# adaLN block with hedgehog attention and a gMLP: `c` moved to another DMA queue, the scale and shift columns reordered, the last output tile split by columns

## The chip, the cores and the metric

The kernel runs on one core of one Trainium2 chip. Its time is device microseconds, the median of the runs shown. The engines are named as in the profile: PE (TensorE matmuls) with PEld (its weight loads), DVE (VectorE), ACT (ScalarE), POOL (GpSimd) and SP (SyncE, which here only issues DMAs). A name with a q behind it (SPq, ACTq) is the engine's sequencer, which issues DMAs. In the lists of DMA packets q1 is the queue of DMAs issued by SP, and q10 that of DMAs issued by ACT.

## The reference

S = 2048 rows, D = 448, 16 heads of 28, FH = 896, all in bf16. Cut to what matters:

```
mod = silu(c) @ w_mod                       # c has 448 numbers; six vectors sa, ca, ga, sb, cb, gb
h   = layernorm(x) * (1 + ca) + sa
q, k, v = h @ wqkv ;  pq, pk = q @ w_phi, k @ w_phi        # per head
phi = [softmax(p), softmax(-p)]
o   = (phi_q @ (phi_k^T v)) / (phi_q . sum(phi_k))
x   = x + ga * (o @ wo)
h   = layernorm(x) * (1 + cb) + sb
z   = gelu(h @ w_in) ; z1, z2 = halves, z2 = layernorm(z2)
x   = x + gb * ((z1 * (w_sp @ z2 + b_sp)) @ w_out)
```

## The kernel before

x is cut into 16 tiles of 128 rows. The program is a list of small steps in the string `ORDER`: each word is one step, optionally with a PSUM slot behind `@` (A0 to A2, B0, B1) and an engine behind `/` (V is DVE, S is ACT, G is POOL, Y is SP). The steps are emitted in exactly that order, so each engine's own order of instructions is the order of the words that it takes part in, and an engine waits only where its next instruction needs something. `consts()` (memsets and the identity) is emitted ahead of the list.

The steps that the change and the prediction touch:

- `ld:c`, `ld:wk`, `ld:x1`, `ld:x0`, `ld:phi`, `ld:wsa`, `ld:wca`, `ld:wq`, `ld:wv`, `ld:x3`: DMA loads, of `c` (one row of 448), the raw key weights, the tiles 1 and 0 of x, w_phi, the columns of w_mod for sa and for ca, the raw query and value weights, the tiles 4 to 7.
- `du:n@slot`: n dummy matmuls of 256 columns on the tile `zero` (line 729). They compute nothing that is used.
- `ct`: turns the row `c` into four columns (four matmuls with one column, line 740). `ce:1` to `ce:4`: silu of it, an exponential on ACT (line 747), then three small operations on DVE (lines 749, 751, 753), which give `scol`.
- `FTk:1`, `FTk:0`: transposes of the key weights on PE (line 822), 8 each; `ETk:1`, `ETk:0`: the copies out of PSUM (826 on ACT, 828 on DVE); `bd`: block-diagonal w_phi on DVE (756); `PFk:m`: key weights times w_phi (849); `EPk:m`: their scaled copies (796, 800).
- `csA`: 16 matmuls of one column that give the shift columns sa from `scol` (764); `esA` copies them (771). `ccA` and `ecA` do the same for ca (764, 768). `FSk`: 16 matmuls of one column with the shift (839).
- `l1s:i`: layer-norm statistics of tile i on DVE (856, 857); `l1e`, `l1r` on POOL (860, 861, 864: epsilon, negated mean, power); `l1a:i`: the normalised tile in `xpad` (867); `X:i`: its four transposes on PE (880); `XE:i`: the copy to `hT`.
- At the end, `oM:t,0,7`: seven matmuls of 448 columns for output tile t (1159), alternately in B0 and B1; `oE:t`: the sum with x on DVE (1162); `oD:t`: the DMA to the output (1165), all on SP.

Behind the list stands a branch on a flag, which skips a general version of the kernel; it is not taken in these runs.

Of the kernel before, what the change touches and what calls it, by code (L numbers as in the profile page):

```python
# [481 lines left out]
ORDER = """tbl du:8@B1 m2b/V ld:wk/Y du:3@A2 m2a/V du:11@A1 ld:c/Y ct@B0 ld:x1/S l1s:1 ld:x0/S l1s:0 m1/G ld:phi/Y ce:1 m3 FTk:1@B1 ce:2 l1e:1,2/G ld:wsa/Y du:2@A0  # L482
l1e:0,1/G FTk:0@A0 ld:wca/Y ce:3 ce:4 bd/V ld:x2/Y ld:wq/Y l1r:0,1 l1a:0/V du:6@A2 X:0@B0 ETk:0/S csA@A2 ETk:1/V PFk:2@B1 l1r:1,2 esA l1a:1/G X:1@A0 XE:0/V
m4 du:2@A2 FSk@B0 ccA@A1 FCk/S PFk:0@B0 ecA XE:1/S EPk:0/V EPk:2/S l1s:3 du:1@A2 PFk:1@A1 EPk:1/S ld:wv/Y l1s:2 PFk:3@A0 l1e:2,4/V EPk:3/S du:2@B0 kM:1@B1
FTq:1@A2 ETq:1/V ld:x3/Y FTq:0@B0 ETq:0/V kM:0@A0 kF:1 FSq@A2 FCq/V kE:1 kS:1 PFq:1@B0 scb kF:0 kE:0 l1r:2,4 l1a:2/G l1a:3/G l1s:4 X:2@B1 SHv@A1 PFq:2@A2
SCv:1/G EPq:1/S XE:2/S l1s:6 PFq:0@B0 SCv:2/G X:3@A0 l1s:5 kM:2@B1 SCv:0/S XE:3/S l1s:7 ld:x4/Y l1s:9 EPq:0/S SCv:3/G l1e:4,8/G l1s:11 kS:0 vM:2@A1 vM:3@B0
EPq:2/S vC:2 ld:wmgb/Y kE:2 PFq:3@A0 EPq:3/S ld:wmga/Y l1s:8 kM:3@A2 kF:2 qM:1@A1 kR:1 ld:x5/S l1r:4,8 vM:0@B1 kR:0 kS:2 kE:3 kF:3 vM:1@A2 l1s:10 qE:1
l1a:4/G gr:1@A0 vC:0 l1s:13 l1a:5/G vC:1 ge:1 gr:0@B1 l1a:7/G kS:3 l1a:6/G vC:3 T1:4,6 kP:0/G T1:6,8 qF:1 kR:2 ge:0 qM:0@A2 qE:0 kP:1/G l1s:12 kM:5@B0
kM:4@B1 kF:4 kP:2/V vM:5@A1 kA:0@A0 kE:4 l1e:8,12/G l1r:8,12 kA:1@A0 kA:2@A0 ld:wo/Y vM:6@B1 l1a:8/G kF:5 kE:5 kR:3 kP:3/V l1s:14 l1s:15 kM:7@B0 l1a:9/G
qF:0 kS:5 vC:6 kM:6@A2 l1a:10/G kS:4 vC:5 l1a:11/G qM:2@A1 kF:6 kR:5 kF:7 kR:4 kE:6 kP:5/V ld:wcb/Y qF:2 T1:8,10 kP:4/V kS:6 kR:6 vM:7@B1 kE:7 T1:10,12  # L490
kA:3@A0 wos:0/G l1e:12,16/G vM:4@A2 l1r:12,16 vC:7 qE:2 l1a:15/G kM:9@B0 kF:9 l1a:12/V l1a:14/G kM:8@B1 l1a:13/V vM:9@A1 kE:9 kS:7 kR:7 kF:8 vC:4 kS:9
kE:8 kS:8 T1:12,14 kM:10@B0 kP:6/G kE:10 kP:7/G kR:8 kF:10 kA:4@A0 kA:5@A0 kM:11@B1 kE:11 T1:14,16 kS:10 vM:10@B0 kF:11 kS:11 kA:6@A0 vC:9 kA:7@A0 kM:12@B1
kP:8/G kR:10 kE:12 kR:9 kP:9/V kR:11 vC:10 kP:10/V kF:12 kS:12 kM:13@A1 kR:12 vM:8@A2 kM:15@B0 vC:8 kF:13 kP:11/G kM:14@B1 ld:wsb/Y kE:13 kS:13 kR:13 kE:14
W:0,6 kF:14 kE:15 kA:8@A0 kA:9@A0 kP:12/V kS:14 vM:11@A1 kF:15 kS:15 kA:10@A0 vM:14@B1 kR:14 vC:11 vM:15@B0 vC:14 vM:12@A2 vM:13@B1 vC:12 kA:11@A0 vC:13
kP:13/G kA:12@A0 kR:15 kP:14/V kP:15/V wos:2/V kA:13@A0 kA:14@A0 vC:15 kA:15@A0 KV:0/V KV:1/V KZ:0 ld:win0/S qM:3@A2 KZ:1 nM:0@A1 qE:3 ld:wout/S nM:1@A0
nX:0 nX:1 qF:3 nC:0 csB@B0 W:0,1 ld:win1/Y nC:1 nS:0 ccB@B1 nT:0 qM:4@A2 qE:4 nA:0/V nT:1 ecB nA:1/V wos:3/V qM:5@A1 nM:2@A0 qF:4 esB nX:2 nM:3@A2 nX:3
FB@B1 wos:1/V nC:2 qE:5 T2:0,1 nC:3 nS:1 FBc/S qF:5 nT:2 nA:2/G wM:0/S@B0 nT:3 SHw:3@B1 wR:0/S SCw:0,3/S T2:1,2 nM:5@A1 nX:5 nM:4@A0 nC:5 nX:4 nC:4 nA:3/V
wQ:0/S wM:1/S@B0 wR:1/S SHw:2@B1 SCw:2,1/S qM:6@A2 SCw:0,0/S SCw:3,1/G nS:2 nT:5 nT:4 T2:2,4 nM:6@A1 wQ:1/V qE:6 nX:6 nM:7@A0 nA:5/G nA:4/V nX:7 SCw:0,2/S
qF:6 nC:6 nC:7 nS:3 nT:7 wM:2/S@B0 wR:2/S wM:3/S@B1 wR:3/S qM:7@A2 wQ:2/S nT:6 wQ:3/S nA:6/V SCw:1,1/V SCw:1,0/V nM:9@A0 T2:4,6 qE:7 nM:8@A1 wM:5/S@B1
nX:8 nX:9 wM:4/V@B0 l2R:0,2/G l2r:0,2 l2a:0/G T3:0,1 l2a:1/V qF:7 nC:8 wR:5/S zM:0@A2 gt nA:7/G l2R:2,4/G nC:9 nS:4 nT:9 nT:8 zG:0 l2r:2,4 l2a:3/G T2:6,8  # L500
wR:4/V l2a:2/G nM:10@A0 T3:1,2 T3:2,4 wQ:5/S nX:10 nA:8/V SCw:3,0/G wM:6/V@B1 wR:6/V nM:11@A1 wQ:4/S nX:11 nA:9/V SCw:2,0/V l2R:4,6/G zM:1@A2 nC:11 nC:10
zG:1 l2r:4,6 nS:5 l2a:5/V wQ:6/S wM:7/V@B1 l2a:4/G yM:0,0@B0 zM:2@A2 yG:0,0 T2:8,10 nT:10 wR:7/V zQ:1/V T3:4,6 W:1,3 zM:3@A0 zG:2 wM:8/V@A2 wQ:7/S l2R:6,8/G
W:0,5 wM:9/V@B1 nT:11 nA:11/V nA:10/V zG:3 wR:8/V zQ:0/S nM:12@A0 nM:13@A2 l2r:6,8 l2a:6/G zM:4@A1 wR:9/V nX:13 nX:12 T2:10,12 zR:0,2/G zQ:3/S wQ:8/S W:1,7
yM:0,4@B0 zG:4 yM:0,1@B1 zQ:4/S nC:13 nM:15@A1 nC:12 zW:0,2 nX:15 yG:0,1 nS:6 nT:13 wQ:9/S nM:14@A2 nX:14 l2a:7/G nT:12 zN:0/V zM:5@A0 yG:0,4 T3:6,8 l2R:8,10/G
l2r:8,10 nA:12/V l2a:9/G nA:13/V nC:15 wM:11/V@B1 zG:5 nC:14 nS:7 l2a:8/G nT:14 zQ:5/S wR:11/V yM:0,5@B0 nT:15 yM:1,3@A0 T2:12,14 yM:1,0@A2 nA:14/G zQ:2/V
nA:15/V yG:0,5 zR:4,6/G zN:1/G wM:10/V@B0 zW:4,6 wM:13/V@A1 wM:12/V@B1 wR:13/V W:2,0 W:0,2 zN:5/G yG:1,0 yG:1,3 yM:1,4@A0 wR:12/V zR:2,4/V zW:2,4 zN:3/G
zN:2/V zM:6@A2 wQ:12/S yM:1,5@B1 wQ:13/S wR:10/V wQ:10/V zG:6 zM:7@A1 T2:14,16 W:2,6 wQ:11/S l2R:10,12/G l2R:12,14/V l2r:10,12 wM:15/V@B0 yG:1,5 zN:4/V
l2a:11/V yM:0,2@A2 wR:15/V zQ:6/S T3:8,10 yM:0,3@B1 W:1,4 W:0,0 zG:7 l2r:12,14 yM:1,1@A1 l2a:13/G yG:1,4 W:0,4 l2a:10/V T3:10,12 yG:1,1 yM:1,2@A0 l2a:12/V
wM:14/V@B0 yG:1,2 zQ:7/V zM:8@A1 yG:0,2 T3:12,14 wR:14/V wQ:14/V yG:0,3 zG:8 wQ:15/V l2R:14,16/V zQ:8/S zR:6,8/G zW:6,8 zN:7/G zM:9@A2 zG:9 zN:6/V l2r:14,16
W:1,1 yM:1,6@B1 yM:0,6@A1 yG:0,6 yG:1,6 zQ:9/V l2a:15/V zM:11@A0 yM:2,5@B0 zM:10@A1 l2a:14/V zG:11 guard@B1 zQ:11/V zG:10 zQ:10/S zM:12@A0 yM:2,4@B1 W:1,5  # L510
zR:8,10/G W:1,0 zG:12 zM:13@A2 zW:8,10 T3:14,16 zR:10,12/G zW:10,12 yG:2,5 yM:3,6@A0 zN:8/V yG:2,4 zN:9/V zG:13 yM:2,2@B1 yG:2,2 yG:3,6 zM:15@A1 yM:3,4@A2
W:1,2 W:2,2 zN:10/V zG:15 zQ:15/S zM:14@A0 zQ:13/V yG:3,4 zN:11/G zG:14 zQ:12/V zR:12,14/V yM:2,6@B0 yM:3,0@A2 yM:3,1@B1 W:1,6 yG:2,6 zQ:14/S tT:1,2/G
yG:3,0 yM:3,2@A0 yM:2,0@A1 zW:12,14 sS:0,1,0,8/V yM:2,1@B0 yM:2,3@A2 yG:3,2 yM:3,5@A0 tT:1,0/V yG:2,0 yG:3,1 zR:14,16/G zW:14,16 zN:14/V zN:15/V yM:3,3@A1
yG:3,5 zN:13/G tT:1,1/V yG:3,3 zN:12/V tT:3,0/V W:0,3 sS:0,2,0,8/V yG:2,3 W:0,7 tT:2,2/V tT:2,1/V ld:bsp/Y gM:1@B1 gG:1 gal P:0,0,1 d:0,0,2 P:0,1,1 tT:2,0/V
d:0,1,1 tT:4,0/V P:0,1,6 d:0,1,3 gM:0@B1 sS:0,3,0,8/V P:0,0,6 P:0,1,5 sS:0,4,0,8/V gG:0 P:0,0,7 d:0,0,1 d:0,0,3 P:0,0,2 d:0,0,4 x:0,0,4/G W:3,4 P:0,0,5
d:0,0,5 W:3,5 W:2,1 P:0,2,1 W:3,1 d:0,0,7 P:0,0,3 P:0,0,4 tT:3,2/V d:0,0,6 d:0,1,2 wts:0/V x:0,0,6/V d:0,0,8 W:2,4 d:0,1,5 wts:1/V x:0,0,8/V tT:3,1/V P:0,1,2
W:3,0 d:0,1,4 W:3,2 wts:2/V tT:4,2/G P:0,2,6 P:0,1,3 x:0,0,7/V wts:3/V d:0,2,1 d:0,2,3 W:2,3 W:2,7 d:0,2,2 x:0,1,4/G P:0,2,7 d:0,1,6 wts:4/V x:0,1,6/V
P:1,0,1 d:1,0,2 P:0,2,2 tT:4,1/V read P:0,2,5 W:3,6 W:2,5 W:3,7 P:0,1,7 d:0,2,4 wts:5/V W:3,3 P:1,1,1 d:0,2,5 wts:6/V P:0,2,3 x:0,2,4/G d:0,2,7 sS:1,1,0,8/V
yG:2,1 sS:1,2,0,8/V d:0,2,6 gM:3@B0 d:0,1,7 gG:3 P:0,1,4 P:0,2,4 x:0,2,7/V x:0,1,7/G d:0,1,8 x:0,2,6/V oM:0,0,7@B0 x:0,1,8/G oE:0 oD:0/Y oM:1,0,7@B1 d:1,1,1
P:1,0,6 d:1,0,1 oE:1 d:1,0,3 d:1,1,2 oM:3,0,7@B0 P:1,0,5 P:1,1,6 oE:3 sS:1,3,0,8/G P:1,0,7 oD:1/Y d:0,2,8 d:1,0,5 d:1,0,7 gM:2@B1 gG:2 P:1,0,2 P:1,1,2  # L520
oM:2,0,7@B1 P:1,0,4 x:1,0,7/V x:0,2,8/G d:1,0,4 P:1,2,1 x:1,0,4/G oM:5,0,7@B0 d:1,1,3 sS:1,4,0,8/V P:1,1,5 d:1,1,5 oE:5 oD:5/Y P:1,1,7 oE:2 d:1,0,8 P:1,0,3
oM:4,0,7@B0 d:1,1,7 d:1,0,6 x:1,0,6/G oD:2/Y d:1,2,1 P:1,2,6 oD:3/Y d:1,2,2 P:1,2,2 oM:6,0,7@B1 P:1,2,7 x:1,0,8/V d:1,2,3 oE:6 P:1,1,3 d:1,1,6 P:1,2,5
oE:4 oD:4/Y oD:6/Y x:1,1,7/G P:1,1,4 x:1,1,6/G oM:7,0,7@B0 d:1,1,4 x:1,1,4/G d:1,2,4 x:1,2,4/G hint d:1,2,5 P:1,2,3 d:1,2,7 d:1,2,6 oE:7 x:1,2,6/G P:1,2,4
d:1,2,8,256,512 oD:7/Y oM:9,0,7@B0 oE:9 oD:9/Y d:1,2,8,0,256 oM:8,0,7@B1 oE:8 x:1,2,7/G oD:8/Y oM:10,0,7@B0 d:1,1,8 oE:10 x:1,1,8/G oD:10/Y oM:11,0,7@B1
oE:11 oD:11/Y x:1,2,8,0,256/G oM:12,0,7@B0 oE:12 oD:12/Y oM:13,0,7@B1 oE:13 oD:13/Y x:1,2,8,256,512/G oM:14,0,7@B0 oM:15,0,7@B1 oE:14 oD:14/Y oE:15 oD:15/Y
# [741 lines left out]
```

## Time and profile before

| | |
|---|---|
| median of 3 runs | 250.34 us (249.0, 250.34, 250.72) |
| the profiled execution | 249.4 us, of which the span is 247.6 us |
| PE busy | 240.5 us, 97% of the span |
| DVE, POOL, ACT busy | 182.5, 116.3, 104.8 us |
| DMA | 25.22 MB, 102 GB/s on the mean |

The span runs from the first instruction to the last event on the core; the execution's own time is 1.8 us longer. PE is busy nearly throughout, so what delays or advances PE at the start moves what stands behind it, and what stands behind PE's last matmul (from 243.2 us on) is a tail in which PE has nothing to do.

### The profile page before, as it was taken

The page shows a single profiled execution, that of the slowest core. Times are in us where ns is not written, and L with a number is a line of the kernel's source. Part 1 is how long each engine was busy: PE and PEld are TensorE (multiplying, and loading weights), DVE is VectorE, ACT ScalarE, POOL GpSimd, SP SyncE. Part 2 cuts the span into 40 slices and gives each one's busy share as a digit, 9 for nine tenths or more (in the row PEclk, how much of TensorE's full clock was granted, in tenths as well). Part 3 has the DMA queues.
Part 4 walks back from the last instruction along what each step waited for, and adds up shares of the span by engine and source line. Part 5 has one row for each costly group of instructions (what it writes and reads, how often), then busy time and mean ns, then how long its engine had stood idle before and what let it go on. Part 6 is the DMA issues. An engine that isn't in the chain of part 4 may idle for free.

```text
span 247.6 us, 4188 instructions
## 1 busy us (share of the span) xinstructions
PE 240.5 (97%) x1533; PEld 126.8 (51%) x1533; DVE 182.5 (74%) x369; ACT 104.8 (42%) x217; POOL 116.3 (47%) x175
## 2 busy tenths in 40 slices
...
GB/s 178 293 217 102 193 86 177 194 113 178 51 72 110 127 162 136 163 158 176 179 177 0 162 181 173 0 1 0 3 0 37 0 0 3 56 0 37 21 95 65
DMA packets 68207, 25.22 MB, mean 102 GB/s; under 512 B 58129, under 2 KB 67602, under 8 KB 68178
## 3 DMA queue, kind: packets, MB, share of 16 engines
...
q8 instruction: 14, 0.23, 0.4%
...
## 4 chain that ended last, share of the span: by engine, by line
PE 85%; POOL 6%; ACT 3%; DVE 2%; DMA 1%; issue 1%; POOLq 0%
PE g_ps L1124 29%; PE o_ps L1159 9%; PE z_ps L1049 7%; PE q_ps L945 6%; PE k_ps L890 5%; PE v_ps L898 5%; PE g_ps L1145 5%; PE z_ps L1078 4%; PE x_ps L1005 4%; PE kvacc L921 3%; PE warm_ps L729 3%; PE num L973 2%; POOL f_zv L1035 1%; DMA f_hT<-f_xpad 1%; DVE f_z2n L1072 1%
## 5 line engine op out<-in xcount | busy, mean ns | idle before, releaser
L1133 DVE TENSOR_TENSOR f_zb<-g_ps,f_zb 128x512 f32<-128x512 f32 (+1 forms) x31 | 20.5, 670 | 17.1 <-PE g_ps L1124 16.7
L1124 PEld LDWEIGHTS <-f_z2n 128*128 128x128 bf16 x192 | 18.8, 98 | 22.7 <-issue 0.3
L1140 POOL TENSOR_TENSOR f_z1T<-f_zb,f_z1T 128x512 bf16<-128x512 f32 (+1 forms) x11 | 12.0, 1102 | 33.6 <-DVE f_zb L1133 33.6
L1049 PE MATMUL z_ps<-f_ar,f_hT 112*128 112x448 bf16 (+1 forms) x128 | 26.6, 352 | 0.0
L1140 POOL TENSOR_TENSOR f_z1T<-f_Sx,f_z1T 128x512 bf16<-128x512 f32 x6 | 8.0, 1332 | 39.3 <-DVE f_Sx L1133 39.3
L1078 PE MATMUL z_ps<-f_hT,f_ar 112*128 112x512 bf16 x112 | 26.1, 379 | 0.0
L1159 PE MATMUL o_ps<-f_wout,f_z1T 128*128 128x448 bf16 x112 | 22.5, 352 | 0.0
L1124 PE MATMUL g_ps<-f_ar 128*128 128x512 bf16 x96 | 22.4, 379 | 0.0
L1081 ACT ACTIVATE f_z1T<-z_ps,f_zb 128x512 bf16<-128x512 f32 x28 | 18.2, 684 | 5.2 <-PE z_ps L1078 5.1
L950 ACT ACTIVATE f_Eq<-q_ps 112x1024 bf16<-112x1024 f32 x16 | 16.3, 1032 | 5.8 <-PE q_ps L945 5.8
L1049 PEld LDWEIGHTS <-f_hT 112*128 112x128 bf16 (+1 forms) x128 | 12.2, 97 | 11.6
L1078 PEld LDWEIGHTS <-f_ar 112*128 112x128 bf16 x112 | 11.0, 98 | 12.6
L893 ACT ACTIVATE f_E<-k_ps 128x448 bf16<-128x448 f32 x32 | 15.8, 555 | 3.8 <-PE k_ps L890 3.7
L989 DVE TENSOR_TENSOR f_ar<-num,f_w 128x896 bf16<-128x896 f32 x16 | 17.0, 1087 | 0.4
L904 DVE TENSOR_REDUCE f_ksum<-f_E 128x32 f32<-128x896 bf16 x16 | 16.9, 1064 | 0.5 <-ACT f_E L893 0.4
L1124 PE MATMUL g_ps<-f_Eq,f_z2n 128*128 128x512 bf16 x72 | 16.5, 379 | 0.0
L1159 PEld LDWEIGHTS <-f_z1T 128*128 128x128 bf16 x112 | 11.0, 98 | 10.7
L1053 ACT ACTIVATE f_zb<-z_ps 128x896 bf16<-128x896 f32 x16 | 14.6, 913 | 4.1 <-PE z_ps L1049 3.8
L1162 DVE TENSOR_TENSOR f_xpad<-o_ps,f_x 128x448 bf16<-128x448 f32 x16 | 9.9, 622 | 8.0 <-PE o_ps L1159 7.9
L945 PE MATMUL q_ps<-f_hT,f_Wq 113*128 113x512 bf16 (+1 forms) x64 | 15.0, 379 | 0.6 <-ACT f_Eq L950 0.6
L1124 PEld LDWEIGHTS <-f_ar 128*128 128x128 bf16 x96 | 9.4, 98 | 11.1 <-DVE f_ar L1102 0.2
L1005 PE MATMUL x_ps<-f_ar 112*128 112x448 bf16 x64 | 14.1, 352 | 0.3 <-DVE f_x L1012 0.3
...
## 6 DMA issues: line engine op xcount, KB each, us to landing
out_dram<-f_xpad SPq DMA_DIRECT2D x16, 112.0 KB, 1.7
f_wm<-in_w_mod_dram SPq DMA_DIRECT2D x4, 406.0 KB, 5.1
f_x<-in_A_x_dram SPq DMA_DIRECT2D x2, 448.0 KB, 7.8
f_wmg<-in_w_mod_dram SPq DMA_DIRECT2D x2, 392.0 KB, 9.9
...
```

What stands on the lines that cost most here:

```text
L904: nc.vector.tensor_reduce(out=ksum[:, i], in_=Er[i % NR][:].rearrange("p s (c f h) -> p (s c) h f", c=4, h=HP), axis=AX.X, op=ALU.add)
L945: nc.tensor.matmul(t[:, u, :], lhsT=Wq[0:KR[m], m, cc * CB:cc * CB + P], rhs=hT[0:KR[m], 4 * st:4 * st + 4, m, :], start=(m == 0), stop=(m ...
L950: nc.scalar.activation(out=Eq[st // 2][0:CB, 2 * c2:2 * c2 + 2, s, (st % 2) * 512:(st % 2 + 1) * 512], in_=ps["q" + str(n)][0:CB, :, :], f ...
L989: nc.vector.tensor_tensor(out=tr[i % 2][:], in0=numv(i)[:, :, :, 0:DH], in1=wr[i // 2 % 2][:, i % 2].unsqueeze(3).to_broadcast([P, 2, H, D ...
L1005: nc.tensor.matmul(t[:, 0, 0:D], lhsT=oT[0:CB, i % 4, cc, :], rhs=wo_s[0:CB, cc, :], start=(cc == 0 and not with_x), stop=(cc == KC - 1))
L1049: nc.tensor.matmul(t[:, hf, 0:D], lhsT=hT[0:KR[m], i, m, :], rhs=win_s[0:KR[m], m, FH + hf * D:FH + (hf + 1) * D], start=(m == 0), stop=(m ...
L1078: nc.tensor.matmul(t[:, 0, :], lhsT=win_s[0:CB, m, fc * P:(fc + 1) * P], rhs=hT[0:CB, 4 * st:4 * st + 4, m, :], start=(m == 0), stop=(m == ...
L1081: nc.scalar.activation(out=stage_b()["z1T"][:, fc, st * 512:(st + 1) * 512], in_=ps["y%d_%d" % (st, fc)][:, 0, :], func=ACT.Gelu_apprx_tan ...
L1124: nc.tensor.matmul(g, lhsT=sta[:, m, :], rhs=mov[:, m, :], start=(m == 0 and i in (1, 6, 7)), stop=(m == 7), skip_group_check=True)
L1133: nc.vector.tensor_tensor(out=o, in0=x, in1=y, op=ALU.add)
L1140: eng.tensor_tensor(out=z, in0=T[r][:, c0:c1], in1=z, op=ALU.mult)
L1159: nc.tensor.matmul(ps["o" + str(t)][:, 0, 0:D], lhsT=later["z1T"][:, FO[n], t * P:(t + 1) * P], rhs=wout_s[:, FO[n], :], start=(n == 0), s ...
```

## The change

Four edits, in `ORDER`, `consts()` and three new steps:

1. `ld:c` moves from SP's queue (second there, behind `ld:wk`) to ACT's queue, ahead of `ld:x1` and `ld:x0`.
2. `ct` stands behind the first 8 dummies instead of behind 22; the dummies `du:3` and `du:11` that stood ahead of it are gone, and a `du:9` stands between `ct` and `FTk:1`. There are five dummies fewer in all.
3. `csA` (called "scale columns" in the change's own words; in the code these are the shift columns) goes ahead of `X:0`. `consts()` zeroes the tile `zero` first and only its first 256 columns, which are all that the dummies read.
4. The last output tile is computed in two parts of columns, 0 to 256 and 256 to 448, each with seven matmuls in a PSUM slot of its own (`oP`), a sum of its own (`oF`) and a DMA of its own (`oG`), the first from ACT and the second from SP.

```diff
-tbl du:8@B1 m2b/V ld:wk/Y du:3@A2 m2a/V du:11@A1 ld:c/Y ct@B0 ld:x1/S l1s:1 ld:x0/S l1s:0 m1/G ld:phi/Y ce:1 m3 FTk:1@B1
+tbl ld:c/S du:8@B1 m2b/V ld:wk/Y ct@B0 m2a/V ld:x1/S l1s:1 ld:x0/S l1s:0 m1/G ld:phi/Y ce:1 m3 du:9@A1 FTk:1@B1
...
-du:6@A2 X:0@B0 ETk:0/S csA@A2 ETk:1/V
+du:6@A1 csA@A2 X:0@B0 ETk:0/S ETk:1/V
...
-oM:14,0,7@B0 oM:15,0,7@B1 oE:14 oD:14/Y oE:15 oD:15/Y
+oM:14,0,7@B0 oP:15,0,256@B1 oE:14 oD:14/Y oP:15,256,448@B0 oF:15,0,256 oG:15,0,256/S oF:15,256,448 oG:15,256,448/Y

 def consts():
+    nc.vector.memset(zero[:, 0:256], 0.0)
     nc.gpsimd.memset(wk_raw[0:CB, :, D:D + 16], 0.0)
...
     nc.vector.memset(one1[:], 1.0)
     nc.vector.memset(warm[:], 0.0)
-    nc.vector.memset(zero[:], 0.0)

+def oP(t, a, b, slot):
+    o = ps["op" + str(a)] = bank(slot, "o_ps")
+    for n in range(FC):
+        nc.tensor.matmul(o[:, 0, 0:b - a], lhsT=later["z1T"][:, FO[n], t * P:(t + 1) * P], rhs=wout_s[:, FO[n], a:b], start=(n == 0), stop=(n == FC - 1))
+
+def oF(t, a, b):
+    nc.vector.tensor_tensor(out=later["ot"][t % 4][:, a:b], in0=ps["op" + str(a)][:, 0, 0:b - a], in1=x_sb[:, t, a:b], op=ALU.add)
+
+def oG(t, a, b, eng):
+    eng.dma_start(out=outv[t][:, a:b], in_=later["ot"][t % 4][:, a:b])
```

The list stands on one line after the change, so line numbers behind it are some 43 smaller there (729 becomes 686).

On ACT, the first instructions of the program before the change; `f_x` is x in SBUF, `f_e` belongs to the silu of c:

```order
L1262 UNCONDITIONAL_BRANCH
L732 ACT_TABLE_LOAD
L732 ACTIVATE f_warm<-f_warm 128x1
L657 DMA f_x<-in_A_x_dram 128x448
L656 DMA f_x<-in_A_x_dram 128x448
L747 ACTIVATE f_e<-ct_ps 112x4
```

And the same place after it:

```order
L1230 UNCONDITIONAL_BRANCH
L689 ACT_TABLE_LOAD
L689 ACTIVATE f_warm<-f_warm 128x1
L612 DMA f_c_row<-in_c_dram 1x448
L614 DMA f_x<-in_A_x_dram 128x448
L613 DMA f_x<-in_A_x_dram 128x448
L704 ACTIVATE f_e<-ct_ps 112x4
```

The load of c now stands ahead of both x tiles on ACT, and both tiles one DMA later.

On PE, the place of the first x tile's transposes (`xt_ps`, step `X:0`) and of the shift columns (`cf_ps`, step `csA`) before the change, from the third of the four transposes to the first of the 16 matmuls; in brackets what the row waits for (a DMA's semaphore, or an engine):

```order
L880 MATMUL xt_ps<-f_ident,f_xpad 128x128
L880 LDWEIGHTS f_xpad
L880 MATMUL xt_ps<-f_ident,f_xpad 128x128
L764 LDWEIGHTS f_wm_119 [waits DMAHW5_49]
L764 MATMUL cf_ps<-f_scol,f_wm_119 128x1 [waits PE_49]
```

And after it, from the last of the 16 matmuls to the second transpose:

```order
L721 LDWEIGHTS f_wm_119
L721 MATMUL cf_ps<-f_scol,f_wm_119 128x1
L837 LDWEIGHTS f_xpad [waits DVE_49]
L837 MATMUL xt_ps<-f_ident,f_xpad 128x128
L837 LDWEIGHTS f_xpad
```

The columns have gone ahead of the transposes, and the wait for DVE (for the normalised tile 0) stands behind them. On DVE the memset of `zero` is the first of three instead of the third, and `f_warm`, for which ACT's first activation waits, is now the last; the rest of DVE's order stays up to the last sum, which becomes two of 256 and 192 columns.

48 lines of the change are left out of this document (3 added, 45 removed).

## Prediction

> **What bounds the kernel now.** I read the page's shares first, then the busy time by stage, and last the chain of work that ended last.
>
> ```profile
> PE 240.5 (97%) x1533; PEld 126.8 (51%) x1533; DVE 182.5 (74%) x369; ACT 104.8 (42%) x217; POOL 116.3 (47%) x175
> 12.10:55.00 42.90, 42.90 (x359) 26.00 (x357) 39.55 (x81) 33.42 (x65) 29.34 (x33) 1.00 0.68 154
> 243.20:247.60 4.40, 0.00 (x0) 0.00 (x0) 0.60 (x1) 0.00 (x0) 0.00 (x0) 0.78 0.20 63
> ```
>
> The last two rows are stages: from, to, length, then the busy time of PE, PEld, DVE, ACT and POOL. From 12.1 to 55 us PE has no idle time, so a shift of the start by some tenths of a microsecond goes on whole; nothing in between can swallow it. From 243.2 on PE is done and the output still has to leave: 4.4 us. The change touches only these two ends. The chain in the first 12 us (start, length, what):
>
> ```profile
> 1.23 4.88 PE warm_ps L729 x22
> 6.11 0.46 PE ct_ps L740 x4
> 6.57 0.62 PE tps L822 x8
> 7.19 0.23 PE warm_ps L729 x2
> ...
> 8.04 0.66 PE warm_ps L729 x6
> 8.70 0.22 PE xt_ps L880 x4
> 8.92 0.38 PE cf_ps L764 x16
> 9.30 0.25 PE pf_ps L849 x4
> 9.55 0.26 PE xt_ps L880 x4
> ```
>
> It is PE throughout, 22 dummies first. But that a chain runs along PE doesn't say that PE alone sets the time: the second `xt_ps` piece (step `X:1`, from 9.55) also needs the normalised tile 1, and POOL delivers it at 8.65 + 0.71 = 9.36:
>
> ```profile
> 4.78 0.63 DVE L856 BATCH_NORM_STATS2 f_st<-f_x 128x6 f32<-128x448 bf16 x1 [2.01 <-DMA f_x<-in_A_x_dram]
> 5.54 0.59 DVE L856 BATCH_NORM_STATS2 f_st<-f_x 128x6 f32<-128x448 bf16 x1
> 6.81 0.17 DVE L749 TENSOR_SCALAR f_e<-f_e 112x4 f32<-112x4 f32 x1 [0.46 <-ACT f_e L747]
> 7.38 0.62 DVE L756 TENSOR_TENSOR f_BD<-f_phi,f_bmask 112x448 bf16<-112x448 bf16 x1
> 8.22 0.62 DVE L828 COPY f_wTk<-tps 112x896 bf16<-112x896 bf16 x1
> 6.91 1.63 POOL L864 TENSOR_TENSOR f_rs<-f_rs,f_mhalf 128x1 f32<-128x1 f32 x2
> 8.65 0.71 POOL L867 TENSOR_SCALAR f_xpad<-f_x,f_nm,f_rs 128x448 bf16<-128x448 bf16 x1
> ```
>
> Statistics of tile 1 (4.78), of tile 0 (5.54), powers on POOL (6.91), the tile (8.65): this row of steps has hardly a gap, starts with the landing of the x tiles, and reaches `X:1` 9.55 - 9.36 = 0.19 us ahead of PE; with some 0.05 us for the hand-over, 0.14 us. **So the start has two nearly equal bounds, and the change relieves one of them (PE) by moving work in front of the other (the x tiles).**
>
> **The start of PE.** The memset that releases PE is first now and half as long.
>
> ```profile
> 0.82 0.06 DVE L686 MEMSET f_warm<- 128x1 f32 x1
> 0.90 0.27 DVE L687 MEMSET f_zero<- 128x256 uint32 x1
> 0.92 0.38 ACTq L657 DMA_DIRECT2D f_x<-in_A_x_dram  x1
> ```
>
> Half of 0.27 is 0.14 (between the 0.06 of the smallest and 0.27): it ends at about 0.92 instead of 1.17, and PE starts at 0.98, 0.25 us earlier. Eight dummies at 4.88/22 = 0.222 end at 2.75. That gain is worth what c allows, because `ct` is next and waits for c. ACT's first DMA row begins 0.04 behind the end of the `f_warm` memset, for which ACT's first activation waits; that memset is now the last of three, so c is issued at about 1.05. When it lands, the trace of before doesn't show (its c came on the other queue, and nothing waited visibly). Bounds: 1.7 us after its issue, the shortest landing of any DMA here, gives 2.8; 3.8 us, the landing of the x tile that was first on ACT's queue, gives 4.9.
>
> ```profile
> f_x<-in_A_x_dram ACTq DMA_DIRECT2D x1, 112.0 KB, 3.8
> f_x<-in_A_x_dram ACTq DMA_DIRECT2D x1, 112.0 KB, 4.1
> out_dram<-f_xpad SPq DMA_DIRECT2D x1, 112.0 KB, 1.7
> q10 hardware_dynamic: 3, 0.00, 3.8%
> q10 hardware_dynamic: 12, 0.01, 11.1%
> ```
>
> The last two rows are ACT's queue from 3.0 to 3.2 us and from 4.4 to 4.6: its first and last packets of the two tiles, issued at 0.92 and 1.34. The first packet moves more than 2 us after the issue, and the second tile counts as landed at 1.34 + 4.1 = 5.44, 0.9 after its last packet. So I take c's packet at 3.1 and its landing at 3.1 + 0.9 = 4.0, nearest to these rows. Then `ct` (0.46) ends at 4.5, nine dummies at 0.222 (2.0) at 6.5, and `FTk:1` starts at 6.5 where it started at 6.57: **the five dummies taken out, 1.1 us, are spent waiting for c.** Over the bounds it starts between 5.3 (the nine dummies again, and the key weights landed at 0.72 + 4.4 = 5.1) and 7.4.
>
> ```profile
> f_wk_raw<-in_A_wqkv_dram SPq DMA_DIRECT2D x1, 392.0 KB, 4.4
> 1.98 1.01 SPq L652 DMA_DIRECT2D f_wm<-in_w_mod_dram  x2
> f_wm<-in_w_mod_dram SPq DMA_DIRECT2D x1, 406.0 KB, 5.1
> ```
>
> From 6.5 PE goes on by the chain's durations: the two groups of transposes and two dummies to 7.97, six dummies to 8.63, the 16 shift columns to 9.01 (their w_mod, issued at 1.98 or earlier, is there by 7.1, and `scol` stands ahead of the row at 7.38), `X:0` to 9.23, the next group to 9.48. The swap of `csA` and `X:0` adds no work; it lets `esA` follow the copy at 8.22 + 0.62 = 8.84 without its wait, and nobody stands behind `esA` before `FSk`, which comes after `X:1`. I cost it at nothing; if tile 0 were late, the columns would fill 0.38 us of the wait.
>
> **The x tiles.** They stand behind c on ACT's queue. Their issue moves by one DMA row (0.38 and the gap, 0.42) and by the 0.13 above: 0.55 us, the upper bound of an ordinary delay. The lower bound is 0: their packets share the 16 DMA engines with the key weights, which get through sooner when ACT's queue starts later, and then leave more of the engines to the x tiles. I take 0.3, the middle, as both rows are equally near. Then the statistics, powers and tile 1 come 0.3 later, at 9.66; `X:1` starts at 9.71 instead of 9.55, **0.16 us later**, after a wait of 0.23 on PE. The small steps of silu on DVE gain nothing: they stand behind the statistics in DVE's order, at 6.81 before and 6.3 + 0.3 = 6.6 now at best. On SP, phi and w_mod are issued 0.43 earlier, on a queue that is full anyway; of the later loads, the tiles 4 to 7 now wait for the semaphore of w_mod's first part (7.1) instead of that of x1, 1.1 us later in issue. They landed at 6.0 + 7.3 = 13.3 and are used from 16.2, so that is covered; without cover it would cost up to 1.1.
>
> ```profile
> 6.03 0.49 SPq L659 DMA_DIRECT2D f_x<-in_A_x_dram  x1
> f_x<-in_A_x_dram SPq DMA_DIRECT2D x1, 448.0 KB, 7.3
> 16.21 0.62 DVE L856 BATCH_NORM_STATS2 f_st<-f_x 128x6 f32<-128x448 bf16 x1
> ```
>
> **The tail.**
>
> ```profile
> 235.95 7.20 PE o_ps L1159 x38
> 243.17 0.62 DVE f_xpad L1162
> 243.83 0.43 SPq L1165 DMA_DIRECT2D out_dram<-f_xpad  x1
> out_dram<-f_xpad SPq DMA_DIRECT2D x1, 112.0 KB, 2.2
> 234.44 0.42 DVE L1133 TENSOR_TENSOR f_zb<-g_ps,f_zb 128x256 f32<-128x256 f32 x1
> 29.02 1.25 PE kvacc L921 x24
> ```
>
> A matmul of 448 columns takes 7.20/38 = 0.189, seven 1.33, so tile 15 starts at 241.83. A dummy of 256 columns takes 0.66/6 = 0.11, so the first part ends at 242.60; 192 columns at the same rate per column take 0.083, above the 1.25/24 = 0.052 that a pair of weight load and short matmul needs here, so the second part ends at 243.18, 0.03 later than now. Its PSUM slot B0 is freed by the sum of tile 14 at 242.5, in time. The sum of 256 columns (0.42) runs under the second part. From 448 columns to 256 the rows fall by 0.20, so 1.04 ns a column, and 192 columns take 0.42 - 0.07 = 0.35: from 243.20 to 243.55 instead of 243.79. The last DMA is issued 0.24 earlier. It lands after 2.2 (the row of the last DMA, at the same place) or 1.7 (most others), so the end moves by -0.24 or -0.74; against that, pieces of 384 bytes are a form that the trace doesn't show, whose extra cost I bound by 0.5, the difference between the two rows, so +0.26 at worst. I take 2.1, near the 2.2: **-0.34 us**. The first part leaves from ACT at 243.1 and is covered by the second.
>
> By a rule of the Trainium skill (DMA: Bandwidth & Descriptors, Specifications) transfers reach line rate from 512 bytes on, and smaller pieces are read, modified and written; the second part has pieces of 384 bytes, the first just 512. If that doubled its packets' time, the -0.34 would become about 0; no row here shows such a piece.
>
> **Sum:** +0.16 - 0.34 = -0.18 us on the profiled execution of 249.4, hence 249.2. That execution lies 0.9 below the median of 250.34, so the same step from the median gives 250.2. The three runs spread over 1.7 us, ten times the step; a measurement of this kernel can tell about 1%, 2.5 us, from no change.
>
> **Rivals.** (1) *The x tiles are delayed by more than the issue.* If the tiles' descriptors are worked off behind phi's or w_mod's, which SP now issues ahead of them, tile 0 lands some 1.0 later instead of 0.3. Against it: x1 and x0 followed each other without a gap on their queue. Price: 0.7 more, 250.9. (2) *PE stays slow longer.* The dummies take 0.222 up to 6.1 us and 0.11 from 7.2 on, at a granted clock that the rows give as 1.00 all along: the array needs some 4.9 us of work to reach its speed. If the gap between 2.75 and 4.0 starts this anew, it is slow until about 9. Eight dummies then cost 0.11 more each (0.9), 16 transposes 0.4 and `X:0` 0.2; 0.23 of this falls into the wait ahead of `X:1`, so 1.3 stays: 251.5, **slower than before**. It decides from a gap that is long enough to undo the start. The Trainium skill (TensorE: Matmul & The Clock Gate, Part 1) says that the clock is released by about 3.4 us of sustained activity in a free-running window and by no count of matmuls; the trace agrees with a slow start, of 4.9 us, and a gap inside such a window speaks for this rival. (3) *c isn't sooner* (lands at 4.9): `FTk:1` at 7.4, PE reaches `X:1` 0.8 later than before: 250.8. It is at the same time the case that the change doesn't do what it says. (4) *Everything lands early:* no delay of the x tiles, so the 0.14 of slack becomes gain, and the last DMA takes 1.7: -0.14 - 0.74, 249.5.
>
> **Chances.** Forecast (within some 0.4 of 250.2) 0.45; rival (1) 0.15, (2) 0.15, (3) 0.1, (4) 0.15. The range: from 249.0, where (4) meets the scatter of the runs below the median, to 251.5, the price of (2). No case reaches 2.5 us by itself; only (2) together with (1) or (3) comes near, and only a chance row of good runs reaches the other side: faster by over 1% 0.03, within 1% 0.93, slower by over 1% 0.04.
>
> **What the profile would show.** PE's first dummy near 1.0; a gap on PE behind the eighth dummy, ended by the DMA of c, about 1.2 us long; `tps` at 6.5; the first statistics on DVE at 5.1; `X:1` behind a wait for POOL near 9.7; the last sum ending 0.4 behind PE's last matmul instead of 0.6, and the last DMA landing 2.1 behind its issue. Wrong would make it: a landing of c far from 4.0, x tiles as early as before or 1 us late, dummies still at 0.22 behind 7 us, a last landing later than 2.2 after its issue.

## The result, and the profile after

| | before | after |
|---|---|---|
| median | 249.61 us (249.0 to 250.72, 6 runs) | 251.78 us (251.49 to 251.88, 6 runs) |
| the profiled execution | 249.4 us, span 247.6 | 251.81 us, span 250.0 |

The changed kernel is slower by 0.8%: ratio 1.0082, 95% interval 1.0061 to 1.0104. The prediction said 250.2 us, a step of -0.2; the step is +2.2, and 251.78 lies above its range. The kernel before scatters by itself: of its 80 executions beside the experiments below, 16 show a mean granted clock of 0.993 or less and took 250.5 us on the median, the other 64 took 249.3.

The chain of work in the first 12 us of the changed kernel (start, length, what):

```profile
1.08 3.39 DMA f_c_row<-in_c_dram
...
4.51 0.53 PE ct_ps L697 x4
5.04 2.03 PE warm_ps L686 x9
7.08 0.75 PE tps L779 x8
7.82 0.44 PE warm_ps L686 x2
...
8.30 0.91 PE tps L779 x8
9.21 1.28 PE warm_ps L686 x6
10.49 0.40 PE cf_ps L721 x16
10.89 0.24 PE xt_ps L837 x4
11.14 0.21 PE pf_ps L806 x4
11.34 0.22 PE xt_ps L837 x4
```

It is PE again, behind a wait for c. But the six dummies that took 0.66 us before take 1.28 now: PE is still slow at 10.5, where it had been fast from 7.2 on. `X:1` (the last row) ends at 11.56 instead of 9.81, **+1.75 us**. On PE's side this is made up of 0.51 from c, behind which the transposes start at 7.08 instead of 6.57, and of 1.28 from the slow PE: from there to the end of the six dummies it takes 3.41 us instead of 2.13. DVE's and POOL's rows of the x tiles (start, length; in brackets idle time and what ended it) show that the other bound moved as far:

```profile
5.29 0.63 DVE L813 BATCH_NORM_STATS2 f_st<-f_x 128x6 f32<-128x448 bf16 x1 [2.51 <-DMA f_x<-in_A_x_dram]
7.31 0.63 DVE L813 BATCH_NORM_STATS2 f_st<-f_x 128x6 f32<-128x448 bf16 x1 [1.17 <-DMA f_x<-in_A_x_dram]
10.29 0.72 POOL L824 TENSOR_SCALAR f_xpad<-f_x,f_nm,f_rs 128x448 bf16<-128x448 bf16 x1
```

Tile 1 of x is 0.51 late (5.29 against 4.78), tile 0 1.77 (7.31 against 5.54), and DVE now waits 1.17 us for it. The normalised tile 1 is there at 10.29 + 0.72 = 11.01 instead of 9.36, 0.33 ahead of PE. **Both bounds of `X:1` moved by some 1.7 us, side by side.**

The tail, by the chain, by the issues of the last DMAs, and by the stage behind PE's last matmul (from, to, length, busy time of PE, PEld, DVE, ACT, POOL, clock, DMA share):

```profile
243.67 1.47 PE o_ps L1127 x14
...
245.16 0.36 DVE f_xpad L1130
```

```profile
244.36 0.33 SPq L1122 DMA_DIRECT2D out_dram<-f_xpad  x1
245.55 0.33 SPq L1133 DMA_DIRECT2D out_dram<-f_xpad  x1
```

```profile
out_dram<-f_xpad SPq DMA_DIRECT2D x1, 112.0 KB, 3.8
out_dram<-f_xpad ACTq DMA_DIRECT2D x1, 64.0 KB, 3.5
out_dram<-f_xpad SPq DMA_DIRECT2D x1, 48.0 KB, 3.0
```

```profile
245.14:250.00 4.86, 0.00 (x0) 0.00 (x0) 0.36 (x1) 0.00 (x0) 0.00 (x0) 0.97 0.24 62
```

The last tile takes PE 1.47 us instead of 1.33 (+0.14). Its last DMA is issued 0.41 behind PE's end instead of 0.68 (-0.27), but lands after 3.0 instead of 2.2 (+0.8). From PE's end to the end of the span there are 4.86 us, before 4.45 (+0.41). So the 2.4 us of the span are 1.75 at the start, 0.09 on the way, 0.14 and 0.41 at the end: **the start and the tail both lost time.**

### The profile page after: what moved, and what is told of

Same layout as the page of the kernel before. It is cut to its first block, busy times and chain, and to the rows that moved or that the text cites. A ratio compares the mean times of both kernels' runs of the same rounds, so it can differ in the third digit from the quotient of the medians.

```text
span 250.0 us, 4195 instructions
## 1 busy us (share of the span) xinstructions
PE 241.0 (96%) x1535; PEld 127.5 (51%) x1535; DVE 183.6 (73%) x370; ACT 104.9 (42%) x217; POOL 115.5 (46%) x175
## 3 DMA queue, kind: packets, MB, share of 16 engines
HBM read 8.87 MB, written 1.84 MB: 43 GB/s over the span
## 4 chain that ended last, share of the span: by engine, by line
PE 83%; POOL 6%; ACT 3%; DMA 3%; DVE 2%; issue 1%; POOLq 0%
PE g_ps L1081 29%; PE o_ps L1116 8%; PE z_ps L1006 7%; PE q_ps L902 6%; PE k_ps L847 5%; PE v_ps L855 5%; PE g_ps L1102 5%; PE z_ps L1035 4%; PE x_ps L962 4%; PE kvacc L878 3%; PE num L930 2%; PE warm_ps L686 2%; POOL f_zv L992 1%; DMA f_c_row<-in_c_dram 1%; DMA f_hT<-f_xpad 1%; DVE f_z2n L1029 1%
## 5 line engine op out<-in xcount | busy, mean ns | idle before, releaser
L1097 POOL TENSOR_TENSOR f_z1T<-f_Sx,f_z1T 128x512 bf16<-128x512 f32 x6 | 7.1, 1183 | 40.5 <-DVE f_Sx L1090 40.5
L1116 PE MATMUL o_ps<-f_wout,f_z1T 128*128 128x448 bf16 x105 | 21.2, 352 | 0.0
L1006 PEld LDWEIGHTS <-f_hT 112*128 112x128 bf16 (+1 forms) x128 | 12.2, 97 | 11.6
L1116 PEld LDWEIGHTS <-f_z1T 128*128 128x128 bf16 x105 | 10.3, 98 | 10.0
L1119 DVE TENSOR_TENSOR f_xpad<-o_ps,f_x 128x448 bf16<-128x448 f32 x15 | 9.2, 622 | 7.3 <-PE o_ps L1116 7.2
```

The costliest lines, as they stand in the source:

```text
L1006: nc.tensor.matmul(t[:, hf, 0:D], lhsT=hT[0:KR[m], i, m, :], rhs=win_s[0:KR[m], m, FH + hf * D:FH + (hf + 1) * D], start=(m == 0), stop=(m ...
L1097: eng.tensor_tensor(out=z, in0=T[r][:, c0:c1], in1=z, op=ALU.mult)
L1116: nc.tensor.matmul(ps["o" + str(t)][:, 0, 0:D], lhsT=later["z1T"][:, FO[n], t * P:(t + 1) * P], rhs=wout_s[:, FO[n], :], start=(n == 0), s ...
```

## The experiments

Theory X: tile 0 of x comes late and sets `X:1`. Theory K: the wait of PE for c keeps PE slow, and that sets `X:1`. Theory T: the split tail costs time. Ratios are against the kernel before, in runs on the same chip (medians 249.3 to 249.35), with 95% intervals.

### The tail alone, the start alone

The tail alone:

```diff
-oM:14,0,7@B0 oM:15,0,7@B1 oE:14 oD:14/Y oE:15 oD:15/Y
+oM:14,0,7@B0 oP:15,0,256@B1 oE:14 oD:14/Y oP:15,256,448@B0 oF:15,0,256 oG:15,0,256/S oF:15,256,448 oG:15,256,448/Y
```

> The start as before, only the last tile in two parts. Theory T (the two last DMAs land 3.0 to 3.5 us after their issue instead of 2.2, so the tail costs time): +0.5 to +0.7 us against before, and the span from PE's last matmul to the end is about 4.9 us instead of 4.4. Rival (the long landings of the changed kernel belong to where instruction fetches happened to fall, not to the split): -0.1 to -0.3 us.

Measured: 250.81 us (10 runs), ratio 1.0059 [1.0041, 1.0077]. With the start of before, the split costs 1.5 us; that it brings time is out. The span grew by 0.75 (median 248.25 against 247.5). In the trace the pieces land after 3.5 us (ACT) and 3.1 us (SP), and from PE's end to the end of the span there are 5.0 us. The rest, 0.8 us, lies outside the span: its runs' times are 2.6 us above their spans on the median, those of before 1.8.

The start alone is the changed kernel with the last output tile undivided, so its diff is the one above, read the other way.

> The whole changed start, the last tile as before. If the start costs what the chain shows (step X:1 ends at 11.56 instead of 9.81), +1.7 to +1.8 us against before. If the end is to blame for more than 0.6 of the 2.2 us, less than +1.5.

Measured: 251.07 us (7 runs), ratio 1.0071 [1.0037, 1.0106], as expected. Tile 0's statistics stand at 7.13 here too. In its trace PE is fast again from about 9.1 on, 1.4 us sooner than in the changed kernel, and the six dummies take 0.97 us; `X:1` still ends at 11.28, since its transposes wait for tile 1 of the normalised x (ready at 10.12 + 0.71 = 10.83). So here the x tiles alone hold `X:1` back, by 1.47 us.

### The two parts of the start

Only the move of c, with the 22 dummies as before:

```diff
-tbl du:8@B1 ... du:11@A1 ld:c/Y ct@B0 ld:x1/S
+tbl ld:c/S du:8@B1 ... du:11@A1 ct@B0 ld:x1/S
```

> Before, with one edit: c first on ACT's queue, ahead of x1 and x0. 22 dummies still stand ahead of ct, so PE has no gap. Theory X (tile 0 is served behind w_mod's first part, which SP now issues ahead of it): x0 lands at about 7, PE waits for tile 0 and step X:1 ends 1.2 to 1.5 later, +1.2 to +1.5 us. Theory K (only PE's slow clock costs time): no gap, so 0 to +0.3 us.

Measured: 252.27 us (4 runs), ratio 1.0117 [1.0057, 1.0177]. The chain runs along tile 0, and PE, which is fast long since, waits for it:

```profile
1.89 5.41 DMA f_x<-in_A_x_dram
```

```profile
10.16 0.40 PE L837 MATMUL xt_ps<-f_ident,f_xpad 128*128 128x128 bf16 x4 [2.01 <-DVE f_xpad L824]
```

`X:1` ends at 11.47, 1.66 late: theory X holds without any wait for c. The time is up by more than that, 3.0 us, since PE slows down again after its idle time. Of the four runs the one with a mean granted clock of 0.999 is up by 1.5 us, as `X:1` is; the others, with 0.985 to 0.993, by 2.4 to 4.1. The stages of the profiled execution (from, to, length, busy time of PE with its count of instructions, clock, DMA share, GB/s):

```profile
12.00:13.00 1.00, 1.00 (x25) 0.59 1.11 336
13.00:14.00 1.00, 1.00 (x11) 0.50 1.10 339
14.00:16.00 2.00, 2.00 (x14) 0.60 1.16 295
```

Only the gap, with c on SP's queue and the shift columns behind `X:0`, both as before:

```diff
-du:8@B1 m2b/V ld:wk/Y du:3@A2 m2a/V du:11@A1 ld:c/Y ct@B0 ... m3 FTk:1@B1
+du:8@B1 m2b/V ld:wk/Y m2a/V ld:c/Y ct@B0 ... m3 du:9@A1 FTk:1@B1
```

> Before, with one edit: 8 dummies ahead of ct and 9 behind it, c second on SP's queue as before, so the x tiles land as before. c lands at about 4.8, so PE idles from about 3.0 to 4.8. Theory K (the gap keeps PE at half speed to about 10): dummies of 0.21 us until then, +1.3 to +1.8 us. Theory X (only the x tiles cost time): 0 to +0.5 us, dummies at 0.11 from 7 us on.

Measured: 251.13 us (8 runs), ratio 1.007 [1.0047, 1.0093]. The x tiles' statistics stand at 5.36 and 6.12, some 0.58 later than before though issued the same, and `X:1` ends at 12.58, +2.77, held by PE: c lands at 5.35, and the dummies are slow to 11.36.

```profile
1.18 4.17 DMA f_c_row<-in_c_dram
...
10.08 1.28 PE warm_ps L686 x6
11.36 0.36 PE xt_ps L837 x4
```

Of the 2.77 us, 1.38 are that the transposes start late (7.95 instead of 6.57: c lands 0.9 later than even in the changed kernel, and nine dummies stand behind it), 1.28 that PE is slow from there to the end of the six dummies (3.41 instead of 2.13), and 0.1 lies in the step itself. So PE's slowness behind a gap is shown without a tile that binds, and theory K holds too; but this run mixes it with a late c, and its 1.8 us are not the price of the gap alone. The delays of X and of K don't add, because both end in the same step.

The changed start with the gap filled:

```diff
-tbl ld:c/S du:8@B1 ... m3 du:9@A1 FTk:1@B1
+tbl ld:c/S du:8@B1 du:9@A1 ... m3 FTk:1@B1
```

> The start of the changed kernel, but all 17 dummies stand ahead of ct and none behind it, so that PE has work until c is there; one undivided last tile. Theory X (tile 0 of x is served behind w_mod and sets X:1): PE is fast from about 6, the key-weight transposes start near 5.5, but tile 0 still lands near 7.2, its statistics stand at 7.2 and X:1 ends at 11 to 11.4; time +1.3 to +1.8 over before. Theory K (the idle gap of PE is what costs, and the tile only fills a wait that PE would have anyway): X:1 ends near 9.7 and the time is that of before, +-0.4.

Measured: 252.32 us (4 runs), ratio 1.0105 [1.0065, 1.0145]. Tile 0 stands at 7.17, `X:1` ends at 11.54: X again. That it is slower than with the gap (+3.0 against +1.8) neither theory had expected. PE is early now and idles, 1.76 and 0.87 us, and is set back for longer than in the kernel with only c moved:

```profile
8.60 0.54 PE L721 MATMUL cf_ps<-f_scol,f_wm 112*128 112x1 bf16 x16 [1.76 <-DVE f_scol L710]
10.01 0.40 PE L837 MATMUL xt_ps<-f_ident,f_xpad 128*128 128x128 bf16 x4 [0.87 <-DVE f_xpad L824]
```

```profile
10.00:11.00 1.00, 0.86 (x9) 0.86 1.13 255
11.00:12.00 1.00, 1.00 (x14) 0.50 1.14 284
...
14.00:16.00 2.00, 2.00 (x10) 0.50 1.14 285
16.00:18.00 2.00, 2.00 (x20) 0.61 0.56 143
```

### What makes tile 0 late

The order of ACT's queue, x1, x0, c, in the changed start:

```diff
-tbl ld:c/S du:8@B1 ... ld:x1/S l1s:1 ld:x0/S
+tbl ld:x1/S ld:x0/S ld:c/S du:8@B1 ... l1s:1
```

> The changed start with the three DMAs of ACT's queue in the order x1, x0, c, and one undivided last tile; only landings are looked at. If the DMAs of SP and ACT are served in the order of their issue, whichever queue they are on, x1 and x0 (issued at 1.1 and 1.5, ahead of w_mod at 1.7) land by 5 and 5.7 as before the change, and c, issued at about 1.9 with two rows of w_mod issued ahead of it or beside it, lands at 6 or later although it is one row of 448 numbers. If each queue has a share of its own, c lands right behind x0, at 5.0 to 5.7, and x0 would not have been late because of w_mod.

Measured (one run): x1 and x0, issued at 1.08 and 1.55, are there at 5.34 and by 6.10; c, issued at 2.03, lands at 5.76. That is close to the second expectation, and c is there 1.5 us ahead of the first part of w_mod (7.3), which was issued 0.33 sooner on SP. But one row of 0.9 KB says little of a load of 112 KB, so it doesn't decide what makes tile 0 late.

The next one does not separate the two causes. With w_mod gone from SP's queue, SP issued `wq` and `wv` at 1.70 and 2.22 in its place, so that x0 stood behind a large load as before:

```diff
-du:8@B1 ... ce:1 m3 du:9@A1 FTk:1@B1 ... ld:wsa/Y ... ld:wca/Y ... ld:x2/Y
+du:8@B1 du:9@A1 ... ld:wsa/S ld:wca/S ld:x2/S ce:1 m3 FTk:1@B1
```

> As e5_gap_filled, but the two parts of w_mod and the tiles 2 and 3 of x are issued on ACT's queue behind x0, at about 2.5, 3.0 and 3.4, instead of on SP's at 1.7 to 2.8; x0 itself is issued at about 2.1 as in the changed kernel. If x0 was late because w_mod was issued ahead of it on the other queue, it lands at about 6.2 instead of 7.3, statistics at 6.2, X:1 ends at about 10.2; time +0.5 over before. If it was late because c stands ahead of it on ACT's queue, it lands at 7.2 again and X:1 ends at 11 or later, time +1.3 to +1.8.

Measured: 254.32 us (4 runs), ratio 1.0186 [1.0146, 1.0227]; tile 0's statistics at 7.25, and PE waits 3.15 us for w_mod besides. By its expectation this speaks for c as the cause; but the large load ahead of x0 had only changed its name, so it tells nothing.

Two that separate them. First the kernel before with w_mod at the head of SP's queue, and no c on ACT's:

```diff
-tbl du:8@B1 m2b/V ld:wk/Y
+tbl du:8@B1 m2b/V ld:wsa/Y ld:wca/Y ld:wk/Y
```

> The kernel before with one thing altered: on SP's queue the two parts of w_mod are issued first, at about 0.7 and 1.2, ahead of the key weights, c and phi; ACT's queue is as before the change (x1 at 0.92, x0 at 1.34, no c on it). Only landings of the x tiles are looked at; PE will wait long for the key weights. If a large load that SP issues first is served first, whatever the queue, x1 and x0 land clearly later than before, x0 at 6.5 or later instead of 5.4. If ACT's queue has its own share of the DMA engines and x0 was late after the change because c stood ahead of it, the tiles land as before, x0 at 5.3 to 5.7.

Measured (one run), SP, ACT and DVE:

```profile
0.72 0.93 SPq L609 DMA_DIRECT2D f_wm<-in_w_mod_dram  x2
```

```profile
1.34 0.45 ACTq L613 DMA_DIRECT2D f_x<-in_A_x_dram  x1
```

```profile
6.86 0.63 DVE L813 BATCH_NORM_STATS2 f_st<-f_x 128x6 f32<-128x448 bf16 x1 [0.61 <-DMA f_x<-in_A_x_dram]
```

x0, issued at 1.34 as before the change, now lands at about 6.8 instead of 5.44, with nothing ahead of it on its own queue but x1.

Second, the kernel with only c moved, and two more loads of c, which nobody reads, between the key weights and phi on SP:

```diff
-ld:wk/Y du:3@A2
+ld:wk/Y ld:c2/Y ld:c3/Y du:3@A2
```

> As e3_c_first_only (c ahead on ACT's queue, everything else as before the change), but with two more loads of the row c, which nobody reads, on SP's queue behind the key weights, so that phi is issued at about 2.0 and w_mod at 2.4 instead of 1.2 and 1.7; x0 is issued at 1.9 on ACT, now ahead of w_mod. If the order of issue decides, x0 lands at 5.8 to 6.3 instead of 7.3, its statistics stand at 6.3 or before, X:1 ends at 10.0 to 10.5 and PE has no second slow phase; time +0.3 to +0.8 over before instead of +3.0. If c ahead of it on ACT's queue is what delays x0, it lands at 7.2 again and the time is +2 to +3.

Measured: 249.54 us (10 runs), ratio 1.0008 [0.9988, 1.0029].

```profile
1.88 4.32 DMA f_x<-in_A_x_dram
```

```profile
2.25 2.55 SPq L611 DMA_DIRECT2D f_wm<-in_w_mod_dram  x2
```

x0 is issued at 1.88 as without the two loads (1.89), behind c on its queue as there, but ahead of w_mod (2.25), and lands at 6.2 instead of 7.3. **Two useless loads win back 2.7 us, because they push w_mod behind x0.** (The 2.7 are a difference of medians of 4 and 10 runs.) With e9 this shows that the order of issue of w_mod and x0, over both queues, decides, and that c ahead on ACT's queue harms by making x0's issue late. In the changed kernel x0 is issued at 2.09 and w_mod at 1.70.

The trace shown is of the slowest of the ten runs (252.19 us). `X:1` ends at 10.39 in it, as expected, but it has a second slow phase, which was not: PE waits 1.26 us for tile 0 ahead of `X:0`, and the clock is 0.50 from about 11.5 to 14.9.

```profile
11.00:12.00 1.00, 1.00 (x25) 0.75 1.14 224
12.00:13.00 1.00, 1.00 (x11) 0.50 1.15 224
```

It also has one wait of 1.3 us in the middle of the kernel.

### What in the tail costs

Split work, one DMA:

```diff
-oF:15,0,256 oG:15,0,256/S oF:15,256,448 oG:15,256,448/Y
+oF:15,0,256 oF:15,256,448 oD:15/Y
```

> The kernel before with the last tile's matmuls and sums in the two parts of columns, but one DMA of the whole tile from SP behind them. If the two DMAs in pieces of 512 and 384 bytes are what makes the split tail slower, this is at or under the time before: the last sum ends some 0.15 sooner, time -0.3 to +0.2. If the split work on PE and DVE costs it (twice as many matmuls, two sums, more instructions at the program's end), it is +0.5 to +1.5.

Measured: 251.16 us (8 runs), ratio 1.0059 [1.0038, 1.008]. Undivided work, two DMAs:

```diff
-oM:15,0,7@B1 oE:14 oD:14/Y oE:15 oD:15/Y
+oM:15,0,7@B1 oE:14 oD:14/Y oE:15 oG:15,0,256/S oG:15,256,448/Y
```

> The kernel before with an undivided last tile (seven matmuls, one sum), whose output leaves in two DMAs of columns, 0 to 256 from ACT and 256 to 448 from SP. If the DMAs are what costs, +0.5 to +1.5 as in e1_tail_only, with landings of 3.0 or more behind the issue; if the split work on PE and DVE costs, 0 to +0.3, with a landing of 2.2.

Measured: 249.94 us (12 runs), ratio 1.002 [1.0003, 1.0037]. Of these 0.6 us its trace shows 0.13 in the tail (4.58 from PE's end to the span's end, against 4.45) and 0.17 at the start, which the edit does not touch (`X:1` ends at 9.98, against 9.81); the rest has no place. The pieces land fast:

```profile
out_dram<-f_xpad ACTq DMA_DIRECT2D x1, 64.0 KB, 2.1
out_dram<-f_xpad SPq DMA_DIRECT2D x1, 48.0 KB, 1.9
```

So the pieces of 512 and 384 bytes are not slow as such. What differs is which DMA ahead of them is slow. In the changed kernel it is that of tile 14 (issued at 244.36, there after 3.8, at 248.2), and both pieces, issued 0.57 and 1.19 behind it, land within 0.4 us of it. Before, it is that of tile 13, one earlier (issued at 241.18):

```profile
out_dram<-f_xpad SPq DMA_DIRECT2D x1, 112.0 KB, 3.9
```

Tile 14's takes 2.9 there, and the last one 2.2; in e12 too it is tile 13's (3.5). Late packets belong to the slow DMAs. Two slices of the changed tail, 247.0 to 247.25 and 247.5 to 247.75 (q1 is SP's queue, q10 ACT's; packets, MB, share of the engines' time):

```profile
q1 hardware_dynamic: 5, 0.00, 15.7%
```

```profile
q10 hardware_dynamic: 8, 0.00, 5.4%
```

At the end a handful of packets takes a sixth of all engine time, and eight of the last nine of ACT's piece, issued at 244.93, move only behind them. The traces show something else beside each slow DMA, which the expectation of e1 had named as a possibility: a packet of the queue that the profile calls instruction. It moves from 242.0 to 242.25 before and from 245.5 to 245.75 in the changed kernel, in both about 1 us behind the issue of the slow DMA:

```profile
q8 instruction: 1, 0.02, 41.4%
```

```profile
q8 instruction: 1, 0.02, 32.5%
```

In the kept traces each of the fifteen output DMAs issued behind 236 us that took 3.2 us or more (in twelve of the traces) was on its way when such a packet moved, 0.8 to 1.6 us behind its issue. With the split work it is the DMA of tile 14 that it meets; in the undivided kernels that show it, that of tile 13, which leaves the last DMA alone. **That the split puts this packet next to the last three DMAs fits all of this, but no run here moves the packet by itself, so the cause of the late landing is not shown.**

The split work's larger cost is not in the span. In e11 the times lie 2.8 us above the spans (2.5 to 3.0), in e12 and in all runs so far but e1 1.8 to 2.0 on the median, the changed kernel included, which has the same tail. Against e1 it has five matmuls fewer. Two runs on that, first e1 with 17 dummies of 332 columns in place of the 22 of 256:

```diff
-du:8@B1 ... du:3@A2 ... du:11@A1
+dv:6,332@B1 ... dv:3,332@A2 ... dv:8,332@A1
```

> As e1_tail_only (start of before, split last tile with its two DMAs), but the 22 first dummies of 256 columns are 17 of 332, the same work of PE in five matmuls fewer, as many matmuls fewer as the changed kernel has against e1_tail_only. In the runs of e1_tail_only and e11_split_one_dma the time lies 2.6 to 2.8 above the span, in all others 1.8 to 1.9. If that part outside the span hangs on the number of PE's instructions in the whole program, it is 1.8 to 1.9 here, the span stays at 248.2, and the time is 250.1 (+0.7 to +0.9 over before). If it hangs on the split work at the end, it stays 2.6 to 2.8 and the time is 250.8 (+1.5).

Measured: 250.2 us (12 runs), ratio 1.002 [1.0001, 1.004], 1.8 us above the span: the 0.8 us outside the span are gone with five matmuls that have nothing to do with the tail. Then the kernel before with seven dummies of one column more:

```diff
-du:8@B1 m2b/V ld:wk/Y du:3@A2
+du:8@B1 m2b/V ld:wk/Y dv:7,1@A0 du:3@A2
```

> The kernel before with seven dummy matmuls of one column more behind the first eight dummies, and nothing else: as many matmuls more as the split adds, with 0.2 to 0.4 of work at most. If the number of PE's instructions in the program decides the part outside the span, it is 2.6 to 2.8 and the time +1.0 to +1.3 over before. If the split work at the end decides it, the part is 1.8 to 1.9 and the time +0.2 to +0.4.

Measured: 250.59 us (7 runs), ratio 1.0067 [1.004, 1.0094]. The part outside the span is 2.06, so only 0.2 of the 0.8 to 1.0 that the number of instructions should bring. The span is 1.0 longer (248.5), of which the seven matmuls are 0.16; the rest is, in the profiled run, a wait in the middle of the kernel that the trace of before does not have; that of e10 has one of 1.3 (waited for: in total, times, longest):

```profile
PE z_ps L1040 <- DMA f_hT<-f_xpad: 1.0, 1, 1.0
```

So the part outside the span depends on more than the work at the end (e13) and on more than the count of PE's instructions (e14). What it hangs on stays open.

### A candidate

22 dummies as before, `zero` cleared first, both x tiles issued ahead of the table load, c on SP, the columns ahead of `X:0`, the tail undivided:

```diff
-tbl du:8@B1 m2b/V ld:wk/Y du:3@A2 m2a/V du:11@A1 ld:c/Y ct@B0 ld:x1/S l1s:1 ld:x0/S
+ld:x1/S ld:x0/S tbl du:8@B1 m2b/V ld:wk/Y ld:c/Y du:3@A2 m2a/V du:11@A1 ct@B0 l1s:1
...
-X:0@B0 ETk:0/S csA@A2
+csA@A2 X:0@B0 ETk:0/S
```

> A candidate: 22 dummies ahead of ct as before the change, the memset of zero first and half as long, c on SP, and both x tiles issued on ACT ahead of the table load and of the activation that waits for a memset; scale columns ahead of X:0; one undivided last tile. Both bounds of X:1 should move up: x1 and x0 are issued at about 0.7 and 1.1 instead of 0.92 and 1.34 and land some 0.2 sooner, PE starts at 1.0 instead of 1.23. X:1 ends at 9.5 to 9.7 instead of 9.81 by both theories; time -0.1 to -0.3, which five rounds can hardly tell from no change. If the order of issue sets the landing, wk (0.72 on SP) and the x tiles now share the DMA engines and wk may land later, up to 5.6, still ahead of its use at 6.3.

Measured: 249.09 us (12 runs), ratio 0.9998 [0.9975, 1.002]: no change against before, and by the two ratios 0.8% better than the changed kernel. PE starts 0.19 sooner and tile 1 comes 0.28 sooner (statistics at 4.50), but tile 0 0.12 later (5.66), and `X:1` ends at 9.89 against 9.81. The memset and the swap of the columns, which are in it, cost nothing that shows.

## Why the prediction was wrong

- **What bounds the kernel** was read rightly: two nearly equal bounds at `X:1`, and a stretch behind it that swallows nothing (1.75 us at `X:1` are 1.84 at the last tile).
- **c** landed at 4.47, within the bounds of 2.8 to 4.9, 0.47 behind the value taken. By itself that is worth half a microsecond: the transposes start at 7.08 instead of 6.57.
- **The step that failed first is the term of the x tiles.** It took 0.3 us from the shift in issue, with 0.55 as the upper bound "of an ordinary delay", and had the normalised tile 1 ready at 9.66; it was ready at 11.01. The issue itself moved by 0.75, since c's row on ACT took 0.55 and not 0.38. Tile 1's landing kept to the bound all the same (0.51). Tile 0 took 1.77, because the change also took c out of SP's queue, which let w_mod be issued at 1.70 instead of 1.98, ahead of x0 instead of behind it. The prediction wrote of this move that phi and w_mod go out 0.43 earlier "on a queue that is full anyway", and cost it at nothing; e9 and e10 show that it costs over a microsecond, and e2 that the x tiles alone then hold `X:1` back by 1.47. Rival (1) named the mechanism; its price of 0.7 and its chance of 0.15 were too low, and the ground against it (no gap between x1 and x0 before) was taken from a program in which both were ahead of w_mod.
- **Rival (2) came true as well**, at the price given: the slow PE costs 1.28 us from the transposes on, in the changed kernel and in e4, where 1.3 was expected. The sum had six dummies at 0.66 and took 1.28. The prediction let (2) together with (1) come near 2.5; but both end in `X:1`, and of two delays side by side only the longer is seen, 1.75.
- **The tail** had the wrong sign: -0.34 expected, +0.55 in the span of the changed kernel. The last DMA is issued 0.27 closer behind PE's end, as expected (0.24 sooner, with PE's end 0.03 later); but PE's end is 0.14 later, so only 0.13 is left. The split matmuls cost 0.14 instead of 0.03: with 192 columns each takes some 0.10 us, and the 0.052 a pair that the estimate bounded them by was from matmuls of another shape. The landing was 3.0, above the range of 1.7 to 2.2 with 0.5 for the form. The form was not the cause: in e12 the pieces landed in 1.9 and 2.1. The rule of the Trainium skill (DMA: Bandwidth & Descriptors, Specifications) that pieces under 512 bytes are read, modified and written shows no cost here, as far as this one row can tell. The estimate went by the landing of the last DMA before the change and took no account of the DMA ahead being the slow one, which it is in the changed kernel; why it is, stays open.
- **What was to be had** from PE alone at the start is by the rows of before 0.14 us, as the prediction said: behind that the x tiles set `X:1`, and this change delays these. No run shows the 0.14 by itself.
